# Mixer with cached attention and a gated MLP: p's low part last, the drain's z1 in other banks, and K, V, Wo and Wq loaded by ScalarE's queue

## The chip, the cores and the metric

The kernel runs on one core of a Trainium2 chip. The metric is the device time of one execution in microseconds. The kernel before took 1814.95 us, the median of three runs (1812.85 to 1819.16).

## The reference, cut to what matters

x is 2048 x 512, normalised by row to xn. Branch A is attention with 32 heads of 128 over the last 512 cached keys and values, without a mask; branch B is a gated MLP with a spatial product over the 2048 rows. All is float32.

```python
xn = _layernorm(x, axis=-1)
# A, W = 512
q = (xn @ wq).reshape(B, Sq, Hq, Dh)            # 32 heads of 128
p = _softmax(einsum("bhqd,bhkd->bhqk", q, k) * Dh ** -0.5)
s = einsum("bhqk,bhkd->bhqd", p, v) (as 2048 x 4096) @ wo
# B, F = 1376, Fh = 688
z = _gelu(xn @ w_in)
z1, z2 = z[..., :Fh], _layernorm(z[..., Fh:])
g = einsum("ts,bsf->btf", w_sp, z2) + b_sp
g = _silu((z1 * g) @ w_out)
return x + s * g
```

## The kernel before, in words

Every product is made of three: each float32 operand is split into a high part (a cast to fp32r on ScalarE, in the trace ACT) and a low part (what is left, subtracted on GpSimd, POOL, or VectorE, DVE), and TensorE (PE) adds high x high, high x low and low x high in PSUM (`mm3`, lines 65 to 67). The product low x low is left out.

**Stages.** First x is normalised and turned, with some of z1's products. Then comes the attention as one loop over steps t (`T0` to `T1`, line 685): 32 heads x 4 blocks of 512 queries are 128 blocks, and each block has four steps of 128 queries, 512 steps in all. After it come z2 (from about 1.45 ms), and last the spatial product, the gate and the output. A tail of the loop, the "drain", has no more queries to project; into its steps the z1 products of the second eight row tiles are put (`DRAIN`, `LAST`, lines 683 and 684).

**A step.** In each step the loop issues, for different blocks: the scores of step t (`score`: three matmuls into a bank of the pool `ps_step`, the row maximum on DVE, the exponential on ACT), the turning of p by 32 x 32 blocks on DVE (`turn`), the split of a turned piece of p (`shares`, eleven steps after its scores: ACT casts pT_h, POOL subtracts pT_l), the product with V two steps later (`pv`, into a bank of the pool `ps_acc`), the output projection by Wo (`outp`, bank of `ps_step`, added into `sacc` on DVE), and a piece of the query projection of coming heads (`q_products`, line 450).

**p's way.** A block's p, turned inside 32 x 32 blocks, is stored to DRAM when its fourth step is turned (`p_dram<-pL`, line 492) and read back in six pieces in the other order of blocks (`pL<-p_dram`, `turned`, line 500). Both are issued by SyncE (SP). The read-backs wait until the store has landed.

**The loads.** K, V and Wo of a head (one 128 x 512 piece each, `load_piece`, line 105) go into the four buffers of the pool `raw`, six steps before they are split; Wq of two heads goes into a pair buffer (`load_q`, line 411) some twelve steps before its first use. Both are issued at the top of a step, on SyncE's queue. A load waits until the piece that held its buffer before has been split. In sixteen steps there are six loads of K, V or Wo and two of Wq. z1's tiles are stored by ScalarE's queue (`z1_out`, line 362).

**What sets the order.** It is written out by hand: the tables `loads`, `todo`, `q_events` and `ends` say which step issues what, and the loop body gives the order inside a step. Every engine takes its instructions strictly in that order. Which bank or buffer a tile gets goes in turn inside its pool; `ps_acc` and `ps_step` have four banks each. A DMA counts on one of eight completion counters, which are given out in turn to all DMAs, whichever queue issues them; a DMA waits for the one before it on the same counter.

Of the kernel before, what the change touches and what calls it, by code (L numbers as in the profile page):

```python
# [8 lines left out]
F32 = mybir.dt.float32  # L9
# [8 lines left out]
P = 128  # L18
# [16 lines left out]
T8 = NT // 2  # L35
# [5 lines left out]
def mixer_kernel(ctx: ExitStack, tc: tile.TileContext, x, wh, w_in, w_sp, b_sp, w_out, out):  # L41
# [8 lines left out]
    nc = tc.nc  # L50
# [12 lines left out]
    def mm3(ps, first, last, lhs, rhs):  # L63
        (lh, ll), (rh, rl) = lhs, rhs
        nc.tensor.matmul(ps, lh, rh, start=first, stop=False)  # L65
        nc.tensor.matmul(ps, lh, rl, start=False, stop=False)  # L66
        nc.tensor.matmul(ps, ll, rh, start=False, stop=last)  # L67

    def cols(pair, lo, hi):
        return tuple(t[:, lo:hi] for t in pair)  # L70
# [12 lines left out]
    ps_acc = psum.enter_context(tc.tile_pool(name="ps_acc", bufs=4, space=PSUM))  # L83
    ps_step = psum.enter_context(tc.tile_pool(name="ps_step", bufs=4, space=PSUM))
# [9 lines left out]
    def x8(shape, dtype=F32R):  # L94
        return xp.tile(shape, dtype, name="x8")

    raw, wt = {}, {}

    def head(h):
        return (h + (H - 2) * (h // H)) % H  # L100

    def load_piece(key, k):
        n = NB if key[0] == "w" else 512
        r = raw[key, k] = (xq.tile([P, 512], F32, name="rawx") if key[0] == "w" else rawp.tile([P, 512], F32, name="raw"))
        nc.sync.dma_start(r[:, :n], w_in[key[1], :, k] if key[0] == "w" else wh[head(key[1]), :, k])

    def load_early(n, cs):
        if (n, "raw") not in raw:
# [81 lines left out]
    def ln_apply(t, i):  # L190
        mean, r = rx[i]
        if i:
            nc.vector.scalar_tensor_tensor(t, t, mean, r.to_broadcast([P, D]), op0=OP.subtract, op1=OP.mult)
        else:
            for k in range(2):
                sl = t[:, k * (D // 2):(k + 1) * (D // 2)]
                nc.vector.tensor_scalar(sl, sl, mean, r, op0=OP.subtract, op1=OP.mult)
# [7 lines left out]
    def ln_flip(i, parts=1):  # L205
        n, j = divmod(i, 4)
        if j == 0:
            for h in range(2):
                X[0][h, n] = block()
        if parts == 1:  # L210
            ps = flip(sacc[:, i, :])
        else:
            ps = ps_step.tile([P, NC, P], F32, name="ps_3")
        rests, rest_of = [], []
        for h in range(2):
            if parts > 1:
                for c in (2 * h, 2 * h + 1):
                    nc.tensor.transpose(ps[:, c, :], sacc[:, i, c * P:(c + 1) * P], ident)
            hi, lo = (quarter(X[0][h, n][:, a], j) for a in range(2))
            nc.scalar.copy(hi, ps[:, 2 * h:2 * h + 2])  # L220
            rests.append((lo, ps[:, 2 * h:2 * h + 2], hi))
        if n == 1:
            p2, y = ps.rearrange("p c q -> p (c q)"), sacc[:, i, :]
            nc.scalar.copy(y[:, :256], p2[:, :256])
            rest_of.append((y[:, 256:], p2[:, 256:], y[:, :256]))
        if parts > 1:
            return rests
        for r in rests:
            rest(nc.vector, *r)
        for r in rest_of:  # L230
            nc.vector.tensor_tensor(*r, op=OP.subtract)
# [107 lines left out]
    def zmm(ps, i, n, cs):  # L339
        for c in cs:  # L340
            mm3(ps, c == 0, c == NC - 1, tuple(x_op(i, a, c) for a in range(2)), cols(wt[("w", n), c], 0, NB))
# [8 lines left out]
                             start=k == 0, stop=k == len(order) - 1)  # L350

    def z1_product(i, n, between=lambda: None):
        ps = ps_acc.tile([P, 512], F32, name="ps_a") if n else ps_step.tile([P, 512], F32, name="ps_3")
        zmm(ps[:, :NB], i, n, range(2))
        between()
        zmm(ps[:, :NB], i, n, range(2, NC))
        return ps

    def z1_out(i, n, ps):
        z = zs.tile([P, NB], F32, name="z1")  # L360
        nc.scalar.copy(z, ps[:, :NB])
        nc.scalar.dma_start(z1_dram[:, i, n * NB:(n + 1) * NB], z)

    def z1_piece(i, n, between=lambda: None):
        z1_out(i, n, z1_product(i, n, between))


    qps, qT, pps, pD, pL, pT, oT, prob, sums = {}, {}, {}, {}, {}, {}, {}, {}, {}

    def where(b):  # L370

        w, r = divmod(b, NBLK // 2)
        p, k = divmod(r, 4)
        return w * H + 2 * p + k // 2, 2 * w + (0, 1, 1, 0)[k]
# [17 lines left out]
    def qproj(b, c):  # L392
        h, qb = where(b)
        if c == 0:
            qps[b] = ps_acc.tile([P, 512], F32, name="ps_a")
        mm3(qps[b], c == 0, c == NC - 1, cols(wt[("q", h), 0], c * P, (c + 1) * P),
            tuple(X[0][c // 2, qb][:, a, c % 2] for a in range(2)))

    def qproj_out(b, c):
        if c == NC - 1:  # L400
            q_out(b, qps.pop(b), True, nc.vector)
# [6 lines left out]
    def load_q(g):  # L408
        r = wraw[g] = wq.tile([P, 2, 512], F32, name="wq", bufs=2)
        for k in range(2):  # L410
            nc.sync.dma_start(r[:, k], wh[head(2 * g + k), :, 0])

    def q_parts(g):
        r = wraw[g]
# [55 lines left out]
    def score(t):  # L470
        b, j = divmod(t, 4)
        ps = ps_step.tile([P, W], F32, name="ps_3")
        mm3(ps, True, True, cols(qT[b], j * P, (j + 1) * P), wt[("h", where(b)[0]), 1])
        if j == 0:
            sums[b] = ap.tile([P, 4], F32, name="sums", bufs=8)
        nm = ap.tile([P, 1], F32, name="nm", bufs=8)
        nc.vector.tensor_reduce(nm, ps, axis=AX.X, op=OP.max, negate=True)  # L477
        prob[t] = ap.tile([P, W], F32, name="prob", bufs=3)
        nc.scalar.activation(prob[t], ps, AF.Exp, bias=nm, accum_out=sums[b][:, j:j + 1])  # L479
# [22 lines left out]
    def shares(b, c):  # L502
        hi = ap.tile([P, 512], F32R, name="pT_h", bufs=4)
        lo = ap.tile([P, 512], F32R, name="pT_l", bufs=4)
        p = pL[b].rearrange("p i (j f) -> p (i j) f", j=4)[:, :, Q * c:Q * c + Q]
        h, l = (t.rearrange("p (i q) -> p i q", q=Q) for t in (hi, lo))
        nc.scalar.copy(h, p)  # L507
        rest(nc.vector if 4 * b + c >= NSTEP - 10 and c % 2 else nc.gpsimd, l, p, h)
        pT[b, c] = (hi, lo)

    def pv(b, c):
        if c == 0:
            pps[b] = ps_acc.tile([P, 512], F32, name="ps_a")
        mm3(pps[b], c == 0, c == 3, cols(wt[("h", where(b)[0]), 2], c * P, (c + 1) * P), pT.pop((b, c)))

    def pv_out(b, c):
        if c == 3:
# [85 lines left out]
    n, t = 0, 28  # L603
    for p in range(4):
        seq, store = later_x(p)
        for k, (f, ks) in enumerate(seq):
            t = max(t + 2, 30 + 13 * n // 5)
# [43 lines left out]
    ps = ps_step.tile([P, 512], F32, name="ps_3")  # L651
# [9 lines left out]
    ps = ps_step.tile([P, 512], F32, name="ps_3")  # L661
# [4 lines left out]
    ps = ps_acc.tile([P, 512], F32, name="ps_a")  # L666
# [16 lines left out]
    LAST = [(i, n) for n in range(2) for i in range(T8, NT)]  # L683
    DRAIN = dict(zip([NSTEP + d for d in (-7, -5, -3, -2, -1, 0, 1, 2, 4, 5, 6, 7, 9, 11, 13)], LAST))
    for t in range(T0, T1):
        for key in loads.get(t, ()):
            if isinstance(key, int):
                load_q(key)
            else:
                load_piece(*key)  # L690
        bq, cq = divmod(t + QL, 4)
        bm, cm = divmod(t - ML, 4)
        bp, cp = divmod(t - PL, 4)
        bo, jo = divmod(t - OL, 4)
        i = t + XL
        if i < T8:
            ln_flip(i)
        if 0 <= bm < NBLK:
            shares(bm, cm)
        for f, args in todo.get(t, ()):  # L700
            f(*args)
        if 0 <= t < NSTEP:
            score(t)
        if i + 2 < T8:
            ln_apply(rows[i + 2], i + 2)
        if t in FILL:
            z1_piece(*FILL[t])
        if 0 <= bq < 4:
            qproj(bq, cq)
        g, s = divmod(t + LEAD, 16)  # L710
        if 0 < g < NG:
            q_products(g, s)
        if 0 <= bp < NBLK:
            pv(bp, cp)
        if 0 <= bo < NBLK:
            outp(bo, jo)
        if t in DRAIN:
            ps = z1_product(*DRAIN[t])
        if 0 <= bq < 4:
            qproj_out(bq, cq)  # L720
        for f, *args in q_events.get(t, ()):
            f(*args)
        if 0 <= bp < NBLK:
            pv_out(bp, cp)
        if t in DRAIN:
            z1_out(*DRAIN[t], ps)
        if 0 <= t - 1 < NSTEP:
            turn(t - 1)
        if t % 4 == 2 and 0 <= t // 4 - 1 < NBLK:
            turned(t // 4 - 1)  # L730
        while late:
            f, *args = late.pop(0)
            f(*args)
        for f, *args in ends.get(t, ()):
            f(*args)

    split_piece(("w", 2), 3, nc.vector)
    ps = z1_product(*LAST[-1])
# [82 lines left out]
    with ExitStack() as st:  # L821
        pl = st.enter_context(tc.tile_pool(name="p2", bufs=1, reuse_waits="tile"))
# [193 lines left out]
```

## Time and profile before

| | |
|---|---|
| median of three runs | 1814.95 us |
| the profiled execution | 1814.89 us, its span 1813.1 us |
| TensorE busy | 1793.2 us, 8,658 matmuls |
| VectorE, ScalarE, GpSimd busy | 1395.4, 1174.4, 1237.8 us |
| granted TensorE clock, mean | 0.998 |
| bytes moved | 394.07 MB, 217 GB/s |
| moved by SyncE's queue, by ScalarE's | 386.60 MB, 5.64 MB |

Times in the trace are microseconds from the start of the span, durations of single instructions partly in ns. A row of waits names the instruction that waits, what released it, and then the sum, the count and the longest wait. PE is TensorE's matmul, PEld its weight load; the name with a q behind it (SPq, ACTq) is an engine's DMA issue, which does not count as busy. A mean of 0.39 us for a matmul is its length in the pipeline: they start closer together than that.

### The profile page before, as it was taken

To read this page: it belongs to the slowest core of one execution; us is meant where nothing else is said; L and a number is where in the kernel's file an instruction comes from. 1 tells how busy PE (TensorE), PEld (TensorE's weight loads), DVE (VectorE), ACT (ScalarE), POOL (GpSimd) and SP (SyncE) were. 2 spreads that over 40 slices of the span, in tenths; PEclk is the share of its full clock that TensorE was granted. 3 is DMA by queue.
4 is the path that set the end of the run, shared out by engine and by line. 5 is a ranking of instruction groups with operands and counts; after the bars stand their busy time and mean duration, and the time that the engine had idled before them with its cause. 6 is when DMAs were issued, how large, how long until landed. Compare 5 with 4: busy or idle time off the path is not lost.

```text
span 1813.1 us, 28712 instructions
## 1 busy us (share of the span) xinstructions
PE 1793.2 (99%) x8658; PEld 1538.0 (85%) x8658; DVE 1395.4 (77%) x2369; ACT 1174.4 (65%) x2625; POOL 1237.8 (68%) x1179
## 2 busy tenths in 40 slices
PE   8999999999999999999999999999999999999999
PEld 7887888888888888788888888888887999999998
DVE  5688988989898988888888888888888556433333
ACT  4777777777777777677777777777776444433332
POOL 2798898898888988788888888888887343000000
PEclk9999999999999999999999999999999999999999
DMA  5578887888888889787777777777778625554532
GB/s 181 176 226 249 245 252 236 266 251 232 253 254 248 250 248 303 256 256 226 232 219 223 219 230 221 225 235 218 226 224 253 219 86 172 171 172 148 182 118 92
DMA packets 181804, 394.07 MB, mean 217 GB/s; under 512 B 24368, under 2 KB 54832, under 8 KB 164496
## 3 DMA queue, kind: packets, MB, share of 16 engines
q1 hardware_dynamic: 177040, 386.60, 70.1%
q10 hardware_dynamic: 4608, 5.64, 0.9%
q8 instruction: 68, 1.11, 0.3%
q14 instruction: 88, 0.72, 0.1%
HBM read 225.42 MB, written 166.72 MB: 216 GB/s over the span
## 4 chain that ended last, share of the span: by engine, by line
PE 89%; DMA 6%; DVE 1%; ACT 1%; POOL 1%; issue 1%; SPq 1%; ACTq 0%; DVEq 0%; POOLq 0%
PE ps_a L450 14%; PE ps L67 12%; PE ps L65 12%; PE ps L66 12%; PE ps_a L66 7%; PE ps_a L67 7%; PE ps_a L65 7%; PE ps_g L65 4%; PE ps_g L67 4%; PE ps_g L66 4%; DMA p_dram<-pL 2%; DMA pL<-p_dram 1%; PE ps_f L67 1%; PE ps_f L65 1%; PE ps_f L66 1%
## 5 line engine op out<-in xcount | busy, mean ns | idle before, releaser
L59 POOL TENSOR_TENSOR pT_l<-pL,pT_h 128x512 fp32r<-128x512 f32 x507 | 656.5, 1298 | 187.6 <-ACT pT_h L507 155.4
L479 ACT ACTIVATE prob<-ps,nm 128x512 f32<-128x512 f32 x512 | 353.9, 691 | 330.4 <-DVE nm L477 320.8
L536 DVE SCALAR_TENSOR_TENSOR sacc<-ps,sums,sacc 128x512 f32<-128x512 f32 x496 | 369.6, 746 | 124.7 <-PE ps L67 118.8
L450 PE MATMUL ps_a<-x,x 128*128 128x512 f32 x1302 | 376.0, 389 | 1.0 <-DVE oT_l L59 1.0
L488 DVE STREAM_TRANSPOSE pL<-prob 128x512 f32<-128x512 f32 x512 | 358.7, 701 | 6.8 <-ACT prob L479 6.8
L477 DVE TENSOR_REDUCE nm<-ps 128x1 f32<-128x512 f32 x512 | 340.0, 664 | 7.0 <-PE ps L67 6.8
L507 ACT CAST pT_h<-pL 128x512 fp32r<-128x512 f32 x512 | 318.2, 622 | 28.1 <-DMA pL<-p_dram 7.6
L450 PEld LDWEIGHTS ps_a<-x,x 128*128 128x128 f32 x1302 | 244.4, 188 | 52.5 <-PE ps_a L450 1.8
L59 POOL TENSOR_TENSOR wl<-raw,wh 128x512 fp32r<-128x512 f32 x186 | 241.3, 1297 | 11.1 <-ACT wh L144 11.1
L66 PE MATMUL ps_a<-pT_l,wh 128*128 128x512 f32 x512 | 200.1, 391 | 3.0 <-POOL pT_l L59 2.8
L65 PE MATMUL ps_a<-pT_h,wh 128*128 128x512 f32 x512 | 199.5, 390 | 1.5 <-ACT pT_h L507 1.4
L65 PE MATMUL ps<-wh,qT_h 128*128 128x512 f32 x512 | 200.3, 391 | 0.5 <-DVE sacc L536 0.5
L67 PE MATMUL ps<-wh,qT_l 128*128 128x512 f32 x512 | 199.8, 390 | 0.0
L67 PE MATMUL ps_a<-pT_h,wl 128*128 128x512 f32 x512 | 199.3, 389 | 0.0
L66 PE MATMUL ps<-wl,qT_h 128*128 128x512 f32 x512 | 199.3, 389 | 0.0
L65 PE MATMUL ps<-wh,oT_h 128*128 128x512 f32 x512 | 199.3, 389 | 0.0
L66 PE MATMUL ps<-wl,oT_h 128*128 128x512 f32 x512 | 199.2, 389 | 0.0
L67 PE MATMUL ps<-wh,oT_l 128*128 128x512 f32 x512 | 199.2, 389 | 0.0
L67 PE MATMUL ps_g<-z_h,x 128*128 128x344 f32 x512 | 161.8, 316 | 0.0
L65 PE MATMUL ps_g<-z_h,x 128*128 128x344 f32 x512 | 161.8, 316 | 0.0
L66 PE MATMUL ps_g<-z_l,x 128*128 128x344 f32 x512 | 161.8, 316 | 0.0
L59 POOL TENSOR_TENSOR x<-wq,x 128x256 fp32r<-128x256 f32 x186 | 138.1, 743 | 1.5 <-ACT x L432 1.5
(203 smaller groups left out, 3179.4 us busy)
## 6 DMA issues: line engine op xcount, KB each, us to landing
p_dram<-pL SPq DMA_DIRECT2D x128, 1024.0 KB, 5.3
pL<-p_dram SPq DMA_DIRECT2D x256, 192.0 KB, 3.8
raw<-wh SPq DMA_DIRECT2D x188, 256.0 KB, 6.5
pL<-p_dram SPq DMA_DIRECT2D x256, 128.0 KB, 3.7
pL<-p_dram SPq DMA_DIRECT2D x256, 64.0 KB, 3.5
wq<-wh SPq DMA_DIRECT2D x62, 256.0 KB, 4.7
x<-w_sp SPq DMA_DIRECT2D x60, 256.0 KB, 5.7
x_dram<-rawx SPq DMA_DIRECT2D x32, 256.0 KB, 6.1
```

What stands on the lines that cost most here:

```text
L59: engine.tensor_tensor(lo, whole, hi.bitcast(F32), op=OP.subtract)
L65: nc.tensor.matmul(ps, lh, rh, start=first, stop=False)
L66: nc.tensor.matmul(ps, lh, rl, start=False, stop=False)
L67: nc.tensor.matmul(ps, ll, rh, start=False, stop=last)
L450: nc.tensor.matmul(qps[g, bank], wt["q", g, k][a][:, c * P:(c + 1) * P], X[g * 2 // H][ORDER[k]][:, b, c], start=first, stop=r == 5, skip_ ...
L477: nc.vector.tensor_reduce(nm, ps, axis=AX.X, op=OP.max, negate=True)
L479: nc.scalar.activation(prob[t], ps, AF.Exp, bias=nm, accum_out=sums[b][:, j:j + 1])
L488: nc.vector.transpose(pL[b][:, :, j * P:j * P + P].rearrange("p a (c q) -> p a c q", q=Q), prob.pop(t).rearrange("p (a c q) -> p a c q", a ...
L507: nc.scalar.copy(h, p)
L536: nc.vector.scalar_tensor_tensor(at, ps, rs, at, op0=OP.mult, op1=OP.add)
```

## The change

Three edits. In the product with V, the matmul that reads p's low part comes third instead of second, so V's low part is read second. The z1 products of the drain with n = 0 take a bank of `ps_acc` instead of one of `ps_step`. And from step 0 on the loads of K, V and Wo, and all loads of Wq, are issued by ScalarE instead of SyncE, at the same places of the loop; four single loads ahead of step 0 stay with SyncE.

```diff
-    raw, wt = {}, {}
+    raw, wt, steps = {}, {}, []
...
-        nc.sync.dma_start(r[:, :n], w_in[key[1], :, k] if key[0] == "w" else wh[head(key[1]), :, k])
+        if key[0] == "w":
+            nc.sync.dma_start(r[:, :n], w_in[key[1], :, k])
+        else:
+            (nc.scalar if steps else nc.sync).dma_start(r, wh[head(key[1]), :, k])
...
-        ps = ps_acc.tile([P, 512], F32, name="ps_a") if n else ps_step.tile([P, 512], F32, name="ps_3")
+        ps = ps_acc.tile([P, 512], F32, name="ps_a") if n or i >= T8 else ps_step.tile([P, 512], F32, name="ps_3")
...
-            nc.sync.dma_start(r[:, k], wh[head(2 * g + k), :, 0])
+            nc.scalar.dma_start(r[:, k], wh[head(2 * g + k), :, 0])
...
-        mm3(pps[b], c == 0, c == 3, cols(wt[("h", where(b)[0]), 2], c * P, (c + 1) * P), pT.pop((b, c)))
+        (vh, vl), (ph, pl) = cols(wt[("h", where(b)[0]), 2], c * P, (c + 1) * P), pT.pop((b, c))
+        nc.tensor.matmul(pps[b], vh, ph, start=c == 0, stop=False)
+        nc.tensor.matmul(pps[b], vl, ph, start=False, stop=False)
+        nc.tensor.matmul(pps[b], vh, pl, start=False, stop=c == 3)
...
     for t in range(T0, T1):
+        if t == 0:
+            steps.append(t)
         for key in loads.get(t, ()):
```

In the trace all weights of a head are named raw<-wh, Wq's pairs wq<-wh. The places in the instruction order where the prediction speaks of the change are shown there, with their rows before and after.

## The prediction

> **What bounds the kernel now.** I read the page first, then the table of stretches, the waits, the DMA issues and the timeline. The page:
>
> ```profile
> span 1813.1 us, 28712 instructions
> PE 1793.2 (99%) x8658; PEld 1538.0 (85%) x8658; DVE 1395.4 (77%) x2369; ACT 1174.4 (65%) x2625; POOL 1237.8 (68%) x1179
> q1 hardware_dynamic: 177040, 386.60, 70.1%
> q10 hardware_dynamic: 4608, 5.64, 0.9%
> ```
>
> TensorE (PE) is busy for 99% of the span: 20 us are left in which it does nothing, and no change that keeps all 8,658 matmuls can win more than these. SyncE's queue (q1) moves nearly all bytes; ScalarE's (q10) moves only the z1 stores. Where the 20 us lie is told by the stretches (length, then busy time of PE, PEld, DVE, ACT, POOL, the clock, the DMA share, GB/s):
>
> ```profile
> 0.00:50.00 50.00, 43.47 (x241) 39.77 (x242) 28.27 (x66) 22.11 (x57) 16.98 (x30) 0.93 0.50 171
> 50.00:100.00 50.00, 48.70 (x223) 39.77 (x222) 34.31 (x59) 35.23 (x87) 37.62 (x42) 1.00 0.62 189
> 100.00:150.00 50.00, 48.09 (x209) 38.65 (x208) 42.13 (x70) 35.14 (x83) 41.89 (x39) 1.00 0.74 230
> 350.00:400.00 50.00, 50.00 (x222) 41.39 (x222) 44.45 (x75) 37.53 (x89) 46.49 (x45) 1.00 0.84 258
> 700.00:750.00 50.00, 47.73 (x208) 38.45 (x207) 41.05 (x70) 32.22 (x76) 38.22 (x37) 1.00 0.86 275
> 1000.00:1050.00 50.00, 50.00 (x222) 41.44 (x221) 43.46 (x72) 37.50 (x88) 44.62 (x42) 1.00 0.79 230
> ```
>
> The start idles 6.5 us, which the change does not touch. Then 50 to 150 us idles 1.3 + 1.9 = 3.2 us and 700 to 750 us idles 2.3 us; in between and afterwards PE is full. ACT is busy 37.5 of 50 us, POOL up to 46.5. What PE waited for inside:
>
> ```profile
> PE ps_a L66 <- POOL pT_l L59: 2.8, 4, 0.8
> PEld ps_a L66 <- POOL pT_l L59: 6.4, 9, 1.3
> 1400.72 0.43 PE L65 MATMUL ps<-x,x 128*128 128x344 f32 x1 [1.59 <-DVE sacc L536]
> ```
>
> The product with V waits for p's low part (pT_l), nine times at the weight load, and one z1 product of the drain waits 1.6 us for its PSUM bank, which VectorE's sum into sacc frees.
>
> **The change part by part.** The profiled execution took 1814.89 us with its span of 1813.1, the median of the three runs is 1814.95, so the sum below starts from 1814.89. About 0.3% (5.4 us) is what a measurement of this kernel can tell from no change: 1809.5 to 1820.4.
>
> *A, p's low part last.* In TensorE's order in the drain, first before, then after (ps_a is the product with V, ps_3_17477 the output product, ps_..17482 a z1 product):
>
> ```order
> L65 MATMUL ps_a_17473<-pT_h_17407,wh2_17116 128x512 [waits Activation_49]
> L66 MATMUL ps_a_17473<-pT_l_17408,wh2_17116 128x512 [waits Pool_49]
> L67 MATMUL ps_a_17473<-pT_h_17407,wl2_17117 128x512
> L65 MATMUL ps_3_17477<-wh3_17012,oT_h_17335 128x512 [waits DVE_49]
> L66 MATMUL ps_3_17477<-wl3_17013,oT_h_17335 128x512
> L67 MATMUL ps_3_17477<-wh3_17012,oT_l_17336 128x512
> L65 MATMUL ps_3_17482<-x8_17180,x8_8451 128x344 [waits Activation_49]
> ```
>
> ```order
> L518 MATMUL ps_a_17473<-pT_h_17407,wh2_17116 128x512 [waits Activation_49]
> L519 MATMUL ps_a_17473<-pT_h_17407,wl2_17117 128x512
> L520 MATMUL ps_a_17473<-pT_l_17408,wh2_17116 128x512 [waits Pool_49]
> L65 MATMUL ps_3_17477<-wh3_17012,oT_h_17335 128x512 [waits DVE_49]
> L66 MATMUL ps_3_17477<-wl3_17013,oT_h_17335 128x512
> L67 MATMUL ps_3_17477<-wh3_17012,oT_l_17336 128x512
> L65 MATMUL ps_a_17482<-x8_17180,x8_8451 128x344 [waits PE_49]
> ```
>
> The wait for POOL moves one matmul later, and z1 takes a bank of the other pool, where it waits for PE itself. One matmul's pace comes from two timeline rows three matmuls apart:
>
> ```profile
> 1317.05 0.39 PE L65 MATMUL ps_a<-pT_h,wh 128*128 128x512 f32 x1
> 1317.72 0.39 PE L65 MATMUL ps<-wh,oT_h 128*128 128x512 f32 x1
> 1359.20 0.39 PE L65 MATMUL ps_a<-pT_h,wh 128*128 128x512 f32 x1
> ```
>
> That is 0.67 / 3 = 0.22 us. Nine waits give at most 9 x 0.22 = 2.0 us; where several follow each other they share one late POOL, so I take 1.0 (0 to 2.0). V's low part, now read second, was split long before and waits for nobody.
>
> *B, z1's bank.* The 1.6 us above go. Next late would be the bank of ps_a; its only other user there is the product with V, which frees a bank every four steps. I take -1.6 (0 to -1.6).
>
> *C, the loads.* 246 issues (184 of K, V and Wo, 62 of Wq) leave SyncE's queue for ScalarE's instruction stream. What one costs ACT is seen on z1's store and the instruction behind it:
>
> ```profile
> 1411.20 0.33 ACTq L362 DMA_DIRECT2D z_dram<-z  x1
> 1411.57 0.62 ACT L507 CAST pT_h<-pL 128x512 fp32r<-128x512 f32 x1 [0.40 <-ACT z L361]
> ACT prob L479 <- DVE nm L477: 320.8, 286, 3.8
> ```
>
> So 0.37 us each, 246 x 0.37 = 91 us. From the rows at 1317.05 and 1359.20, sixteen steps of the loop take 42.15 us; in these ACT gets 8 issues, 3.0 us, and has 42.15 x 12.5 / 50 = 10.5 us idle. Three issues in one step are 1.1 us, as long as ACT's mean wait for the row maximum (320.8 / 286). Cost on the path: 0; without that cover it would be 3.0 us in 42.
>
> The dearer part is what the issues wait for and who waits for them. The DMA completion counters (DMAHW0 to 7) are handed out in turn to both queues, and a DMA waits until the one before it on its counter has landed. SyncE's order before (p_dram is the store of a block's turned p, pL its read-back), then after:
>
> ```order
> L492 DMA p_dram_3953<-pL_3839 128x2048 [waits DVE_49]
> L105 DMA raw_3957<-wh 128x512 [waits DMAHW2_49,Pool_49]
> L105 DMA raw_3990<-wh 128x512 [waits DMAHW3_49,Pool_49]
> L318 DMA x_dram12_104<-rawx_3852 512x1x128 [waits DMAHW4_49]
> L318 DMA x_dram13_105<-rawx_3854 512x1x128 [waits DMAHW5_49]
> L500 DMA pL_3839<-p_dram_3953 32x3x512 [waits DMAHW6_49,DMAHW1_49]
> ```
>
> ```order
> L495 DMA p_dram_3953<-pL_3839 128x2048 [waits DMAHW3_49,DVE_49]
> L321 DMA x_dram12_104<-rawx_3852 512x1x128 [waits DMAHW6_49,Activation_49]
> L321 DMA x_dram13_105<-rawx_3854 512x1x128 [waits DMAHW0_49,Activation_49]
> L503 DMA pL_3839<-p_dram_3953 32x3x512 [waits DMAHW3_49,DMAHW1_49,Pool_49]
> L503 DMA pL_3839<-p_dram_3953 32x512 [waits DMAHW2_49]
> ```
>
> The two loads are gone from the row, and the store waits on counter 3, which in the built program was last given to raw_3957: a store that went ahead of this load now waits until it has landed. In ScalarE's order the same happens to ACT itself. Before and after, at the softmax of one step (prob) and the cast of the next p (pT_h):
>
> ```order
> L479 ACTIVATE prob_4602,sums_4491<-ps_3_4596,nm_4600 128x512 [waits DVE_49,Activation_49]
> L507 CAST pT_h_4621<-pL_4267 128x512 [waits PE_49,Pool_49]
> L432 CAST x8_751<-wqs_4315 128x256
> L479 ACTIVATE prob_4634,sums_4631<-ps_3_4627,nm_4632 128x512 [waits DVE_49,Activation_49]
> L522 CAST oT_h_4648<-ps_a_4533 128x4x4x32 [waits PE_49]
> ```
>
> ```order
> L482 ACTIVATE prob_4602,sums_4491<-ps_3_4596,nm_4600 128x512 [waits DVE_49,Activation_49]
> L108 DMA raw_4616<-wh 128x512 [waits Pool_49]
> L414 DMA wq_4618<-wh 128x512 [waits DMAHW0_49]
> L414 DMA wq_4618<-wh 128x512
> L510 CAST pT_h_4621<-pL_4267 128x512 [waits PE_49]
> ```
>
> Three loads have come between; Wq's first waits on counter 0, which raw_4548 took two steps before, and the cast of p for TensorE stands behind it. How long depends on how fast a load lands, for which the DMA issues (count, KB each, us from issue to landing) give three figures at the same 256 KB (the last three rows show z1 and p):
>
> ```profile
> raw<-wh SPq DMA_DIRECT2D x188, 256.0 KB, 6.5
> wq<-wh SPq DMA_DIRECT2D x62, 256.0 KB, 4.7
> raw_z<-w_sp SPq DMA_DIRECT2D x4, 256.0 KB, 3.0
> z_dram<-z ACTq DMA_DIRECT2D x32, 172.0 KB, 2.9
> p_dram<-pL SPq DMA_DIRECT2D x128, 1024.0 KB, 5.3
> pL<-p_dram SPq DMA_DIRECT2D x256, 192.0 KB, 3.8
> ```
>
> 6.5 us behind SyncE's other traffic, 3.0 us alone. The loads' other wait, for POOL to have split the piece that held the buffer, is carried over from SyncE, where it was short each time:
>
> ```profile
> SPq L105 <- POOL wl L59: 23.6, 42, 0.9
> ```
>
> I cost it at nothing: ACT's 10.5 us in 42 cover 0.9. The place of raw_4548 in ACT's stream is behind the query's activation, that of wq_4618 behind a softmax:
>
> ```profile
> 361.11 0.59 ACT L381 ACTIVATE qT_h<-ps_a 128x512 fp32r<-128x512 f32 x1
> 364.99 0.69 ACT L479 ACTIVATE prob<-ps,nm 128x512 f32<-128x512 f32 x1
> 367.71 0.69 ACT L479 ACTIVATE prob<-ps,nm 128x512 f32<-128x512 f32 x1 [1.13 <-DVE nm L477]
> ```
>
> They lie 3.9 us apart, so ACT would stand 6.5 - 3.9 = 2.6 us at the long landing, 0.8 us at the 4.7 of Wq, not at all at 3.0. The next softmax waited 1.13 us for DVE anyway, so 1.5, 0 and 0 us are left. From 150 to 700 us there are 550 / 42.15 = 13 groups of sixteen steps: 0 to 13 x 1.5 = 19.5 us. I take 0.7 a group, between the long landing and the others: +9. After 750 us, where the DMA share is lower (0.79 in the row at 1000 against 0.84 at 350), I expect no loss. The store that is held has more room. Its way in the trace:
>
> ```profile
> 316.00 0.34 SPq L492 DMA_DIRECT2D p_dram<-pL  x1
> 320.75 3.04 SPq L500 DMA_DIRECT2D pL<-p_dram  x6
> 332.38 0.62 ACT L507 CAST pT_h<-pL 128x512 fp32r<-128x512 f32 x1
> ```
>
> raw_3957 is reached by ACT at about 316, so the store is held by 3.0 to 6.5 us. The last read-back went out at 323.4 and lands 3.8 later, at 327.2, 5.2 us ahead of the first cast that needs it (332.38). A hold of 3.0 is covered; one of 6.5 makes the cast 1.3 late, which the two steps (5.3 us) between cast and product take up. Cost: 0, up to the 1.3 per group counted inside the 19.5 above.
>
> In 50 to 150 and 700 to 750 us there is no such room, and there the loads' departure from SyncE's ring helps the read-backs, while the new waits harm them: between -5.5 (all idle time goes) and +5.5 (it doubles). I take 0, since the same bytes pass the same DMA engines.
>
> Sum: -1.0 - 1.6 + 9 + 0 = +6.4, so 1814.89 + 6.4 = 1821.3 us.
>
> The Trainium skill's page "DMA: Bandwidth & Descriptors", section "Issuing engines are not separate DMA queues", says that DMAs started by ScalarE, SyncE or GpSimd run on the same 16 engines and interleave, and that a second issuing engine saves only issue time. By that rule the landing stays at 6.5 and the sum would be -2.6 + 19.5, 1831.8; the trace has too few transfers on ScalarE's queue in a full stretch to decide.
>
> **The rivals.**
>
> *Held reads reach TensorE (slower still).* If loads on ScalarE's queue land in 6.5 us or more and the stretches without room double their idle time, the sum is -2.6 + 19.5 + 5.5 = +22.4: 1837.3. For it: POOL at 46.5 of 50 us cannot catch up what ACT loses. Against it: PE has been full there, with 5 us of room.
>
> *The ring is relieved (faster).* In 700 to 750 us the store waits in SyncE's ring behind fetches and loads:
>
> ```profile
> 717.39 0.57 SPq L492 DMA_DIRECT2D p_dram<-pL  x1
> 724.74 2.66 SPq L500 DMA_DIRECT2D pL<-p_dram  x6
> ```
>
> 7.4 us from store to read-back instead of 5.3. Without loads ahead of it the 5.5 us of idle time may go: -2.6 - 5.5 = -8.1, 1806.8. It decides if loads on the other queue land within 3.9 us, so that no hold is felt. Against it: Wq's 4.7.
>
> *All holds are covered (no change to tell).* Only A and B are left: 1812.3. That the change does not do what it says is excluded by the rows of the order above.
>
> **How the numbers follow.** Forecast, 1816 to 1827 us: 0.42, of which 0.12 lies below 1820.4. Slower still: 0.25. Covered: 0.18. Relieved: 0.15. So faster 0.15, same 0.18 + 0.12 = 0.30, slower 0.30 + 0.25 = 0.55. The range leaves out about half of the relieved case and the upper part of the slower one, a tenth each: 1808 to 1840.
>
> **What would show it.** Right: in 150 to 700 us PE is no longer full, the casts of p (L510) wait for read-backs and for ACT's own DMA issues, and SyncE's stores and read-backs wait for raw; the row of the drain's z1 wait is gone, and the weight loads wait less for pT_l. Wrong: PE's busy time in 350 to 400 stays at 50.00, or moved loads land within 4 us, or the idle time of 50 to 150 us is gone.

## The result, and the profile after

The changed kernel takes 1819.24 us (median of 22 runs, 1813.08 to 1823.11) against 1816.19 us of 22 runs of the kernel before: ratio 1.0016, interval 1.0009 to 1.0022, some 3 us slower. The forecast was 1821.3, and its likeliest case 1816 to 1827. By the bound of 0.3% named there this counts as no difference, which the prediction had given 0.30, against 0.55 for slower; the many runs do tell it from none. In one of the experiments below (lead7) two of ten executions took 2336 and 4672 us, the others 1816 to 1823, and its median leaves the two out.

The page of the changed kernel, first the engines, then the two queues:

```profile
span 1817.7 us, 28573 instructions
PE 1796.3 (99%) x8658; PEld 1537.3 (85%) x8658; DVE 1396.4 (77%) x2369; ACT 1176.0 (65%) x2625; POOL 1238.4 (68%) x1179
q1 hardware_dynamic: 141616, 322.10, 54.6%
q10 hardware_dynamic: 40032, 70.14, 14.7%
```

ScalarE's queue (q10) now carries 70 MB, 64 more than before. The busy time of every engine is the same to within some 3 us. Where TensorE lost time is read from the stretches (length, busy time of PE with the matmuls begun, then PEld, DVE, ACT, POOL, clock, DMA share, GB/s). Two of the kernel before, which the prediction's rows don't cover:

```profile
150.00:700.00 550.00, 548.06 (x2423) 450.68 (x2422) 494.33 (x846) 414.99 (x972) 489.94 (x471) 1.00 0.85 251
1350.00:1450.00 100.00, 98.18 (x488) 84.92 (x487) 70.59 (x114) 59.55 (x133) 58.19 (x50) 1.00 0.74 233
```

And of the changed kernel:

```profile
50.00:150.00 100.00, 95.68 (x427) 77.87 (x426) 76.88 (x129) 71.41 (x171) 80.72 (x82) 1.00 0.68 215
150.00:700.00 550.00, 547.98 (x2418) 449.15 (x2417) 492.87 (x842) 410.51 (x960) 484.05 (x466) 1.00 0.81 248
350.00:400.00 50.00, 50.00 (x222) 41.41 (x221) 44.67 (x75) 36.23 (x86) 44.84 (x43) 1.00 0.79 252
700.00:750.00 50.00, 45.97 (x189) 35.51 (x188) 37.16 (x63) 30.74 (x73) 35.65 (x34) 0.97 0.88 283
1350.00:1450.00 100.00, 99.92 (x491) 85.92 (x490) 72.45 (x119) 61.27 (x137) 60.35 (x52) 1.00 0.73 231
```

The count of matmuls shows losses that the modelled busy time hides. From 150 to 700 us, where the forecast put +9 us, 5 of 2423 are missing, 1.1 us at 0.22 each. In 700 to 750 us 19 of 208 are missing, 4.2 us; in 50 to 150 us 3 of 430. Not all of the 4.2 us is waiting: the granted clock is 0.97 in that row, and in windows of 0.5 us it is 0.50 from about 727.6 to 730.8 us, right behind gaps of TensorE of 1.8 and 0.6 us. Half of these 3.2 us is 1.6 us (an estimate). The drain (1350 to 1450) idles 0.1 us instead of 1.8: that is z1's bank. So one profile against the other says: gained in the drain, lost at 700 us, and next to nothing where it was forecast.

What the engines waited for in the changed kernel; SyncE's queue first (L495 is the store of p, L503 its read-back), then ScalarE:

```profile
SPq L503 <- DMA raw<-wh: 149.2, 47, 8.1
SPq L495 <- DMA raw<-wh: 43.2, 11, 4.9
SPq L495 <- DMA wq<-wh: 25.3, 21, 2.7
SPq L503 <- DMA wq<-wh: 6.7, 6, 2.1
ACT pT_h L510 <- DMA pL<-p_dram: 23.0, 16, 4.6
ACT pT_h L510 <- issue: 5.3, 8, 1.6
ACT pT_h L510 <- PE ps L67: 26.0, 23, 4.2
```

The same rows of the kernel before:

```profile
SPq L492 <- DMA raw<-wh: 8.2, 14, 0.9
SPq L500 <- DMA raw<-wh: 4.4, 6, 1.7
ACT pT_h L507 <- DMA pL<-p_dram: 7.6, 4, 2.7
ACT pT_h L507 <- PE ps L67: 6.6, 3, 4.3
```

SyncE's stores and read-backs of p, which had waited 12.6 us for loads, now wait 224 us: they stand at the completion counters of loads that ScalarE issued. Not all of this is added time, since they wait for less else: all rows of the two lines together grow from some 704 to 870 us. The casts of p wait for their read-back 16 times instead of 4, and in 150 to 700 us 7 times instead of never.

ScalarE has no row of waiting for a load, but its own issues do delay it. The row "issue" shows only 5.3 us of this. The last row, put down to TensorE, has grown from 3 waits to 23, and in the timeline most of these casts start just when a load's issue ends. In all, 32 idle stretches of ScalarE (29.6 us, 13.9 of them in 150 to 700 us) end within 0.12 us of the end of one of its load issues. Much of this is covered: the softmax's wait for the row maximum (DVE nm) falls from 320.8 to 275.7 us.

The block that the prediction followed, in the timeline of SyncE and then of ScalarE:

```profile
318.13 0.34 SPq L495 DMA_DIRECT2D p_dram<-pL  x1
324.91 4.06 SPq L503 DMA_DIRECT2D pL<-p_dram  x6
315.11 0.33 ACTq L108 DMA_DIRECT2D raw<-wh  x1
332.93 0.62 ACT L510 CAST pT_h<-pL 128x512 fp32r<-128x512 f32 x1
```

The store goes out 2.1 us later (316.00 before), the six read-backs take 4.06 us instead of 3.04, and the last leaves at 329.0 instead of 323.8, 5.2 us later. That was about the room ahead of the first cast: with the median landing of 3.8 us it is there at about 332.8, and the cast starts at 332.93, against 332.38 before. The room is used up and TensorE has lost nothing yet.

### The profile page after: what moved, and what is told of

Read it like the earlier page. It is cut to its first block, busy times and chain, and to the rows that moved or that the text cites. A ratio compares the mean times of both kernels' runs of the same rounds, so it can differ in the third digit from the quotient of the medians.

```text
span 1817.7 us, 28573 instructions
## 1 busy us (share of the span) xinstructions
PE 1796.3 (99%) x8658; PEld 1537.3 (85%) x8658; DVE 1396.4 (77%) x2369; ACT 1176.0 (65%) x2625; POOL 1238.4 (68%) x1179
## 4 chain that ended last, share of the span: by engine, by line
PE 95%; DMA 2%; POOL 1%; DVE 1%; issue 1%; ACT 0%; ACTq 0%; SPq 0%; POOLq 0%; DVEq 0%
PE ps_a L453 15%; PE ps L65 13%; PE ps L67 12%; PE ps L66 12%; PE ps_a L520 6%; PE ps_a L518 6%; PE ps_a L519 6%; PE ps_g L66 4%; PE ps_g L65 4%; PE ps_g L67 4%; PE ps_a L66 2%; PE ps_a L65 2%; PE ps_a L67 2%; PE ps_f L67 1%; PE ps_f L66 1%; PE ps_f L65 1%
## 5 line engine op out<-in xcount | busy, mean ns | idle before, releaser
L482 ACT ACTIVATE prob<-ps,nm 128x512 f32<-128x512 f32 x512 | 352.9, 689 | 285.3 <-DVE nm L480 275.7
L453 PEld LDWEIGHTS ps_a<-x,x 128*128 128x128 f32 x1302 | 244.5, 188 | 51.9 <-PE ps_a L453 0.9
```

The costliest lines, as they stand in the source:

```text
L453: nc.tensor.matmul(qps[g, bank], wt["q", g, k][a][:, c * P:(c + 1) * P], X[g * 2 // H][ORDER[k]][:, b, c], start=first, stop=r == 5, skip_ ...
```

## The experiments

Every kernel is compared by its ratio with the kernel before, run beside it. The medians belong to different groups of runs, in which the kernel before itself had medians of 1814.59 to 1816.58 us. In the table, "casts held" is the row of the casts of p waiting for their read-back, and the last columns are the matmuls begun in two stretches of the profiled execution.

| kernel | median us | ratio, interval | casts held, us (times) | 150 to 700 us | 700 to 750 us |
|---|---|---|---|---|---|
| before | 1816.19 | | 7.6 (4) | 2423 | 208 |
| changed | 1819.24 | 1.0016, 1.0009 to 1.0022 | 23.0 (16) | 2418 | 189 |
| ab_alone | 1814.03 | 0.9990, 0.9979 to 1.0001 | 14.4 (7) | 2423 | 192 |
| ab_again | 1812.64 | 0.9997, 0.9986 to 1.0007 | 4.4 (3) | 2421 | 208 |
| a_alone | 1814.94 | 1.0000, 0.9987 to 1.0014 | 14.1 (5) | 2423 | 197 |
| wq_on_act | 1825.83 | 1.0057, 1.0042 to 1.0071 | 34.3 (17) | 2393 | 183 |
| kvo_on_act | 1823.80 | 1.0052, 1.0033 to 1.0070 | 51.9 (21) | 2379 | 184 |
| tight_on_sync | 1817.90 | 1.0012, 1.0002 to 1.0022 | 25.1 (15) | 2414 | 185 |
| wq_on_gpsimd | 1814.97 | 0.9996, 0.9987 to 1.0004 | 6.9 (7) | 2418 | 202 |
| kvo_on_gpsimd | 1818.16 | 1.0022, 1.0011 to 1.0033 | 18.9 (9) | 2406 | 198 |
| lead7 | 1820.36 | 1.0021, 1.0010 to 1.0033 | 24.4 (14) | 2407 | 189 |
| lead5 | 1831.02 | 1.0079, 1.0065 to 1.0093 | 45.6 (26) | 2366 | 188 |
| lead7_sync | 1817.74 | 1.0004, 0.9994 to 1.0015 | 17.0 (11) | 2402 | 194 |
| x_fetch_on_gpsimd | 1815.65 | 1.0003, 0.9994 to 1.0011 | 12.5 (9) | 2415 | 198 |

**The drain's edits alone (ab_alone).** All loads go back to SyncE:

```diff
-            (nc.scalar if steps else nc.sync).dma_start(r, wh[head(key[1]), :, k])
+            nc.sync.dma_start(r, wh[head(key[1]), :, k])
...
-            nc.scalar.dma_start(r[:, k], wh[head(2 * g + k), :, 0])
+            nc.sync.dma_start(r[:, k], wh[head(2 * g + k), :, 0])
```

> Edits A (p's low part last) and B (z1's bank) alone, all loads back on SyncE. Theory 1 (in the two traces the drain gained 1.6 us, 150 to 700 us lost 1.4, and 50 to 100 and 700 to 750 us together lost about 8 where 100 to 150 won 3): the loads cost about 5 us, nearly all of it in the stretches without room, and the drain's edits win 1.6 to 2.6. Then this kernel takes 1816.2 - 2 = 1814 us, ratio 0.9985 to 0.9992, with 700 to 750 us idle for about 2.3 us as before. Rival 2: the order of the products with V is what moved the waits in 700 to 750 us (they now stand at pT_h); then this kernel idles there for 4 us as the changed one does and is not faster than before, ratio 1.000 to 1.002. Rival 3: idle time there differs from one execution to the next and A and B are worth nothing: ratio 1.000.

The time is as theory 1 has it, 0.9990. The stretch at 700 us is not: with all loads on SyncE it began 192 matmuls, not 208. So most of what the two first profiles differ by at 700 us is no proof against the loads.

**Half of the loads each (wq_on_act, kvo_on_act).** One of the two lines above goes back to SyncE, the other stays.

> A and B, and only Wq's 62 loads on ScalarE's queue; K, V and Wo on SyncE's. In the changed kernel Wq's loads landed after 9.5 us in 690 to 745 us (5.3 before) and a read-back there waited for one. Theory 1a: it is Wq, two loads back to back behind each other's counters, that holds the read-backs: then most of the 5 us is here, 1817.5 us or more (ratio 1.0005 or over). Theory 1b: it is K, V and Wo, three times as many and earlier in the block: then this one is within 1 us of A and B alone, about 1814.5 to 1815 (ratio 0.999 to 0.9995).

> A and B, and only the 184 loads of K, V and Wo on ScalarE's queue; Wq on SyncE's. Theory 1a (Wq's loads hold the read-backs): about 1814.5 to 1815.5 us, ratio 0.999 to 0.9997. Theory 1b (K, V and Wo do): about 1818 to 1819, ratio 1.001 to 1.0015. Rival 4, that the loss is ScalarE's issue time and so in proportion to the issues (184 of 246): three quarters of 5 us, 1817.5, ratio 1.0008, and as much in 800 to 1300 us as elsewhere.

Both theories took the whole to be the sum of its halves. It isn't: each half costs more than the whole (1.0057 and 1.0052 against 1.0016). The waits of SyncE and the long stretch, with only Wq on ScalarE:

```profile
SPq L503 <- DMA wq<-wh: 129.6, 39, 6.0
ACT pT_h L510 <- DMA pL<-p_dram: 34.3, 17, 5.2
```

```profile
150.00:700.00 550.00, 544.89 (x2393) 443.98 (x2392) 488.47 (x837) 407.71 (x952) 479.93 (x462) 1.00 0.82 245
```

With only K, V and Wo there:

```profile
SPq L495 <- DMA raw<-wh: 101.6, 29, 5.1
SPq L503 <- DMA raw<-wh: 24.4, 20, 4.0
ACT pT_h L510 <- DMA pL<-p_dram: 51.9, 21, 5.5
```

```profile
150.00:700.00 550.00, 542.70 (x2379) 442.71 (x2378) 484.96 (x830) 405.05 (x952) 478.68 (x461) 1.00 0.79 244
```

Here is a loss of the size that the forecast described, from 150 to 700 us: 30 matmuls (6.6 us) and 44 (9.7 us). The second is from an execution of 1830.06 us, 6 us above its median. In the one case the loads hold read-backs, in the other mostly stores. The cost is not in proportion to ScalarE's issues (rival 4): 62 issues cost as much as 184. Nor does it follow the time for which ScalarE stands at them: the idle stretches that end with a load's issue are 9.6 us with Wq alone and 2.1 us with K, V and Wo alone, against 29.6 us in the changed kernel, which loses least.

**The loads back on SyncE where the casts have no room (tight_on_sync).**

```diff
-            nc.scalar.dma_start(r[:, k], wh[head(2 * g + k), :, 0])
+            (nc.scalar if steps else nc.sync).dma_start(r[:, k], wh[head(2 * g + k), :, 0])
...
-        if t == 0:
-            steps.append(t)
+        steps[:] = [t] if 32 <= t < 232 or t >= 268 else []
```

> The changed kernel with its loads on SyncE's queue again while steps 0 to 31 and 232 to 267 run (about 60 to 143 us and 680 to 783 us, where the casts of p have no room), and on ScalarE's in the other 444 of 512 steps. Theory 1: the time of A and B alone, 1814 to 1815.5 us (ratio 0.9988 to 0.9996), 700 to 750 us idle for about 2.3 us. The forecast's own term (ScalarE is held at the counters in each group of sixteen steps from 150 to 700 us): the loss stays but for a tenth, 1818 to 1819 us, ratio 1.001 to 1.0015.

1.0012: theory 1 falls. The time is the one given for the forecast's own term, but the trace does not show that term: 9 matmuls (2.0 us) are missing from 150 to 700 us. The stretch at 700 us began 185 matmuls though its own loads were on SyncE. An argument, not shown: the stretches ahead of it had used up the room, so that it began with none.

**Counters of their own (wq_on_gpsimd, kvo_on_gpsimd).** Two theories were left. C: the DMAs on SyncE wait at the counters of loads that another queue lets land late. S: a load on a second queue runs beside the stores and read-backs instead of behind them and slows them. In the built program GpSimd's DMAs count on semaphores of another set (DMASW), and in the traces no store or read-back of p waits for such a load.

```diff
-            nc.scalar.dma_start(r[:, k], wh[head(2 * g + k), :, 0])
+            nc.gpsimd.dma_start(r[:, k], wh[head(2 * g + k), :, 0])
```

kvo_on_gpsimd changes the line of K, V and Wo in the same way, from step 0 on.

> As the kernel with only Wq's 62 loads on ScalarE's queue (1825.8 us, ratio 1.0057), but they go out on GpSimd's queue, whose DMAs have completion counters of their own (DMASW). The bytes still run beside SyncE's. Theory C (counters: read-backs of p on SyncE wait for the landing of the load that had their counter before): the read-backs no longer wait for Wq, and the time is that of A and B alone plus what GpSimd's own issuing takes, 1813 to 1818 us, ratio 0.9985 to 1.0015. Theory S (sharing: a load on a second queue runs beside the stores and read-backs of p instead of behind them, and slows them): as on ScalarE, 1824 to 1828 us, ratio 1.0045 to 1.007.

> A and B, and the 184 loads of K, V and Wo on GpSimd's queue, whose DMAs have completion counters of their own; on ScalarE's queue the same loads took 1823.8 us (ratio 1.0052). Theory C (counters): no store or read-back of p waits for raw any more. GpSimd pays for the issues: with Wq on its queue its busy time rose from 1238.4 to 1270.5 us for 62 issues, 0.52 us each, so 184 cost it 95 us in 1360, 2.9 us in 42, of which it has 42.15 x 3.5 / 50 = 3 to 7 us free; 1814 to 1820 us, ratio 0.9985 to 1.002. Theory S (sharing of the DMA engines): 1823 to 1828 us, ratio 1.004 to 1.007, with stores of p that land as late as on ScalarE's queue. GpSimd at its limit would show as more waits for pT_l.

With Wq, the time is that of theory C and not of theory S: 0.9996 instead of 1.0057, 11 us back, while the bytes still run on a second queue. The move also takes the issues out of ScalarE's stream, which this run does not separate from the counters. SyncE has no row of waiting for Wq any more, and the casts and the long stretch are nearly as before (the page's engines and the landing of its DMA issues, then ScalarE's waits, then the stretch):

```profile
PE 1792.4 (99%) x8658; PEld 1536.4 (85%) x8658; DVE 1395.7 (77%) x2369; ACT 1174.1 (65%) x2625; POOL 1270.5 (70%) x1241
wq<-wh POOLq DMA_DIRECT2D x62, 256.0 KB, 5.6
```

```profile
ACT pT_h L510 <- DMA pL<-p_dram: 6.9, 7, 1.6
```

```profile
150.00:700.00 550.00, 547.15 (x2418) 449.54 (x2418) 493.12 (x844) 412.52 (x966) 501.55 (x494) 1.00 0.83 251
```

K, V and Wo come back by some 5 us (1.0052 to 1.0022), not wholly: they stay 4.5 to 5.8 us above A and B alone (0.9990 and 0.9997). Here ScalarE's issues can hardly have been the cost, with 2.1 us of standing. Two things are seen there that counters don't explain. Stores land after 5.7 us, and TensorE's weight loads wait 14.6 us for GpSimd; with A and B alone it is 5.0 and 5.1. First the rows of kvo_on_gpsimd (DMA issues, waits of the weight loads):

```profile
p_dram<-pL SPq DMA_DIRECT2D x128, 1024.0 KB, 5.7
```

```profile
PEld ps_a L520 <- POOL pT_l L59: 14.6, 20, 1.8
```

And the same of A and B alone:

```profile
p_dram<-pL SPq DMA_DIRECT2D x128, 1024.0 KB, 5.0
```

```profile
PEld ps_a L520 <- POOL pT_l L59: 5.1, 8, 1.3
```

Whether the rest is sharing or GpSimd's own load was not separated.

**The place of the loads (lead7, lead5, lead7_sync).**

```diff
-    def plan(key, k, t, lead=6):
+    def plan(key, k, t, lead=7):
...
-        loads.setdefault(max(T0, t0 - 12), []).append(g)
+        loads.setdefault(max(T0, t0 - 13), []).append(g)
```

lead5 has 5 and 11; lead7_sync is lead7 with the loads on SyncE.

> The changed kernel with every load of K, V, Wo and Wq one step (2.63 us) earlier in the program. In the built program the DMA that takes a load's counter next (eight DMAs later) is then a store or read-back of p within two steps in 3 cases, against 35 in the changed kernel. Theory C: read-backs find their counters free; 1813 to 1816 us, ratio 0.9985 to 1.000, and SyncE waits for raw and wq much less than the 239 us of the changed kernel. Theory S: as many bytes beside the same transfers, so as the changed kernel, 1818 to 1820, ratio 1.001 to 1.002.

> The changed kernel with every such load one step later: the next on its counter is a store or read-back of p within two steps in 52 cases. Theory C: more held read-backs, 1822 to 1830 us, ratio 1.003 to 1.008. Theory S: as the changed kernel, 1818 to 1820, ratio 1.001 to 1.002, unless the pieces themselves come late for their split, which would show as GpSimd or ScalarE waiting for raw.

> A and B, the loads one step earlier as in the run before last, but on SyncE's queue: tells what the earlier place does without ScalarE's queue. On one queue a load has mostly landed before the DMA behind it reaches its turn, so the place should matter little: the time of A and B alone within 1.5 us, 1813 to 1816 us, ratio 0.998 to 1.000. If this one is as much faster than A and B alone as the earlier loads on ScalarE are faster than the changed kernel, the earlier place and not the counters is what helps.

lead7 is a miss. Its place, chosen by counting steps in the built program, freed little; the stores and read-backs waited 177 us for loads in 102 waits, after 224 us in 85:

```profile
SPq L503 <- DMA raw<-wh: 109.6, 49, 5.6
SPq L503 <- DMA wq<-wh: 45.0, 37, 3.2
SPq L495 <- DMA wq<-wh: 15.5, 12, 1.8
SPq L495 <- DMA raw<-wh: 7.0, 4, 4.8
```

The count of two steps was too short: with three steps it is 50 cases here and 109 in the changed kernel. lead7_sync missed its range too, by little (1.0004), and from 150 to 700 us it began 2402 matmuls, 21 fewer than A and B alone, with no load on ScalarE's queue; so the place itself costs something there. Against it the move to ScalarE costs 1820.36 - 1817.74 = 2.6 us by the medians and 3.1 us by the ratios, about as much as at the old place (3.5 to 4.7). lead5 came out as theory C said, 1.0079, with the largest number of held casts and these waits, and the long stretch:

```profile
SPq L503 <- DMA raw<-wh: 176.1, 84, 7.6
ACT pT_h L510 <- DMA pL<-p_dram: 45.6, 26, 4.7
```

```profile
150.00:700.00 550.00, 542.21 (x2366) 437.61 (x2365) 482.48 (x826) 403.80 (x944) 474.88 (x457) 1.00 0.80 240
```

No row shows a wait for a late piece. The one row of ScalarE waiting for a load, 1.0 us, is a cast of p that stands behind Wq's issue and doesn't read the load: ScalarE was held at its issue. The later place on SyncE's queue was not run, so what of the 1.0079 belongs to the place alone is open.

**The fetches of x at 700 us (x_fetch_on_gpsimd).** A version to beat both: A and B, and the crowded stretch cleared.

```diff
-        nc.sync.dma_start(X[w][k][:, n % 2, n // 2].bitcast(F32), xd[w, k][:, n % 2, n // 2])
+        nc.gpsimd.dma_start(X[w][k][:, n % 2, n // 2].bitcast(F32), xd[w, k][:, n % 2, n // 2])
```

> A and B alone, and the 28 fetches of x (256 KB each) that fill 690 to 745 us go out on GpSimd's queue. There the stores and read-backs of p stand behind these fetches in SyncE's ring and TensorE idled for 3 to 7 us in the profiled executions. If the ring is what delays them, the store lands sooner than the 6.1 to 6.5 us measured there, the idle time falls to 0 to 2 us and the time to 1810 to 1812 us, ratio 0.996 to 0.998. If it is the sharing of the DMA engines (busy for 0.86 of the time), nothing changes: 1814, ratio 0.999.

No gain, 1.0003. The stores of 690 to 745 us land later, not sooner. First this kernel, then A and B alone (again):

```profile
p_dram<-pL SPq DMA_DIRECT2D x5, 1024.0 KB, 8.3
x<-x_dram POOLq DMA_DIRECT2D x17, 256.0 KB, 6.3
```

```profile
p_dram<-pL SPq DMA_DIRECT2D x5, 1024.0 KB, 7.0
x<-x_dram SPq DMA_DIRECT2D x18, 256.0 KB, 5.3
```

The read-backs of p (192 KB) land there after 5.0 us instead of 3.5. In the other traces with all of p, x and the loads on SyncE (before, A alone, A and B twice) the stores take 6.9 to 7.4 us and the read-backs 3.3 to 3.9. What had stood ahead of the store in one ring now runs beside it: the effect of theory S is seen where the stretch is full.

**A alone, and A and B once more (a_alone, ab_again).** a_alone leaves out B and the move of the loads.

> Only the order of the three products with V is changed (p's low part last); z1's bank and the loads are as before. The prediction's term A: -1.0 us (0 to -2.0), so ratio 0.9989 to 1.000, the drain's z1 wait of 1.6 us still there, and TensorE's weight loads wait less for pT_l than the 6.4 us of before. If A is worth nothing: ratio 1.000, and A and B alone (0.999) owed its gain to z1's bank.

> A and B alone once more, to say whether this version is faster than before: the first time its ratio was 0.999 with an interval from 0.9979 to 1.0001, and A alone was 1.000. If z1's bank is worth the 1.6 us by which the drain's idle time fell in the trace, the ratio is again 0.9985 to 0.9995; if the first figure was chance, 0.9998 to 1.001. Its trace also tells whether 700 to 750 us idles differently with the same loads on the same queue (3.2 us in the profile of before, 6.8 in the first run of A and B alone): if it lies more than 1 us from 6.8, that stretch differs by itself.

A alone is 1.0000; its weight loads wait 5.6 us for pT_l instead of 6.4. The second run of A and B gives 0.9997 after 0.9990. Both lie below 1, and neither interval excludes it. The stretch at 700 us began 208 matmuls here and 192 the first time, with the same instructions. First ab_alone, then ab_again:

```profile
700.00:750.00 50.00, 46.80 (x192) 37.34 (x191) 38.56 (x65) 30.61 (x74) 35.66 (x35) 0.93 0.81 274
```

```profile
700.00:750.00 50.00, 47.90 (x208) 38.43 (x207) 41.24 (x69) 33.20 (x80) 37.62 (x37) 1.00 0.85 279
```

TensorE's busy time differs by 1.1 us only; the larger part is the clock. In ab_alone TensorE waits 3.1 us for one cast of p, and around the end of this wait the granted clock falls to 0.50, for some 6.8 us (729.4 to 736.2); half of it is 3.4 us. In ab_again the same wait is 1.5 us and the clock stays at 1.00. So a wait that is a little longer can cost more than itself; how long it must be these runs don't settle. One profile against one says nothing about less than 16 matmuls (3.5 us) there. Still, all six kernels with loads on ScalarE begin 183 to 189, and all others 192 to 208.

## Why the prediction was right, and which term was not

The sum was -1.0 (A) - 1.6 (B) + 9 (loads from 150 to 700 us) + 0 (stretches without room) = +6.4 us; measured are about +3.

- **A, -1.0.** Below what the runs resolve: 1.0000, with an interval of 2.5 us to either side.
- **B, -1.6.** Right in the trace. The row of the z1 product waiting 1.6 us for sacc is still there with A alone, and gone with A and B; the drain's idle time falls from 1.8 to 0.1 us in the changed kernel. The row with A alone, from its timeline:

```profile
1400.73 0.43 PE L65 MATMUL ps<-x,x 128*128 128x344 f32 x1 [1.73 <-DVE sacc L539]
```

A and B together were forecast at -2.6 and gave ratios of 0.9990 and 0.9997 (-1.8 and -0.5 us).
- **The loads, +9.** By time the move costs 1.0016 over 0.9990 to 0.9997, 3.5 to 4.7 us: the sign is right, the size half. From 150 to 700 us, where the term was put, the profile lost 5 matmuls, 1.1 us. The step that failed is "ACT would stand 2.6 us at the long landing". The loads land sooner on ScalarE's queue, and the pair of the same group that was costed shows it (DMA issues with the us to landing, then ScalarE's timeline):

```profile
raw<-wh ACTq DMA_DIRECT2D x184, 256.0 KB, 4.6
wq<-wh ACTq DMA_DIRECT2D x62, 256.0 KB, 6.0
```

```profile
360.84 0.33 ACTq L108 DMA_DIRECT2D raw<-wh  x1
365.74 1.10 ACTq L414 DMA_DIRECT2D wq<-wh  x1
366.87 0.46 ACTq L414 DMA_DIRECT2D wq<-wh  x1
```

The load of Wq took 1.10 us to issue where the next took 0.46, so ScalarE stood there for 0.6 us, near the 0.8 us that the prediction gave for a landing of 4.7 us. The cast of p behind it starts at 367.37, 1.7 us later than before, and the softmax behind that at 368.20, 0.5 us later, in a timeline that was 0.3 us late already: nearly all is covered. By its own second figure, the term would have been 0. What the traces show in its place is the other side of the same coupling, SyncE's stores and read-backs, with 224 us of waiting at loads, and the casts held behind them. That this, and not ScalarE's issues, is the whole price of the changed kernel is argued, not shown. The prediction had this mechanism, with the right block and the right room (5.2 us), and costed it at 0 since the room covers a hold. It does so in that block. But the 7 casts that waited in 150 to 700 us, and the loss when a half of the loads moves, show that the room was not ample.
- **The stretches without room, 0 (-5.5 to +5.5).** The ones that lost most in the profile of the changed kernel, some 4 us at 700 us; how much of this one execution differs by, and what the clock does there, is above. That two wrong sizes, +9 and 0, still put the time into the likeliest range is in part luck.
- **What would show it.** The casts do wait for read-backs and for ScalarE's own issues, SyncE does wait for raw, and the drain's z1 wait is gone. But the weight loads wait for pT_l 7.8 us, not less than the 6.4 of before (5.1 to 5.6 in the three runs of A alone and of A and B), and one sign of being wrong came: in 350 to 400 us TensorE is still busy for 50.00 us (222 matmuls, as before). The landing of 4.6 us lies near the 4 us that were named as another.
- **A reading.** TensorE was not quite full where the prediction says so: before the change it idled 1.9 us from 150 to 700 us, besides the 1.8 us of the drain.

The Trainium skill's page "DMA: Bandwidth & Descriptors", section "Issuing engines are not separate DMA queues", has the queues share the same engines. The runs agree where the stretch is full: the store's 8.3 us beside fetches on another queue against 7.0 behind them. The sum by that rule (1831.8) did not come, for the loads' landing did not stay at 6.5 us: out of the ring in which they stood behind SyncE's traffic it was 4.6 us. The place in the loop matters as well as the ring: issued one step earlier on SyncE's queue (lead7_sync), the loads of K, V and Wo landed after 4.6 us too.

What stays open is why half of the move costs more than the whole. Which store or read-back shares a counter with which load follows from the count of DMAs in the built program and the time at which each queue gets there, and the neighbours do change. Counted in the built programs, within three steps, Wq's 62 loads stand ahead of 42 read-backs and 1 store when moved alone, and of 8 and 27 when all loads move; K, V and Wo stand ahead of 37 read-backs and 38 stores alone, and of 61 and 13 with all. But the whole has more such neighbours (109 against 43 and 75), and its stores and read-backs wait longer for the moved loads (224 us against 131 and 126), and yet it costs least. So neither the number of neighbours nor the sum of SyncE's waits tells the cost. It goes roughly with the time for which casts are held by their read-backs (23.0 us against 34.3 and 51.9), but which neighbour holds which cast was not followed. That Wq's cost comes from its place among SyncE's counters or in ScalarE's stream, and not from its bytes on a second queue, is shown on GpSimd's queue, where about 1 us of it is left at most (0.9996 against 0.9990 and 0.9997).

## What to carry to other kernels

When a DMA moves to another queue, list who waits at its completion counter afterwards: on one queue the wait is nearly free, since what stands ahead in the ring has mostly landed (12.6 us here), and across two queues it couples the engines (224 us). Look at the room of those who are made to wait, not only at the engine that issues. And before a stretch of two single profiles is compared, run the same kernel twice and read the granted clock: here it differed by 3.5 us with nothing changed.

## What the runs showed that had not been expected

- Parts of a move don't add up: +11.8 us for Wq alone and +9.8 for K, V and Wo alone, over A and B alone (1814.03), against 3.5 to 4.7 for both.
- 62 loads on GpSimd's queue cost it 1270.5 - 1238.4 = 32 us of busy time, 0.52 us each, and nothing that the time shows; they were 11 us faster there than on ScalarE's.
- A load of K, V or Wo (256 KB) lands after 6.5 us in SyncE's ring and 4.6 us on ScalarE's at the same places of the loop, but Wq's pairs, issued right behind a load of Wo, K or V, took 6.0 there against 4.7.
